# A spectral filter's middle stage: one sum per step on GpSimd, the last steps in another order, step 15 in two PSUM tiles, no transposes

## The chip, the cores and the metric

The kernel runs on one core of a Trainium2 chip. Its engines work beside each other, each through its own queue in program order: TensorE (PE, with its weight loads PEld) multiplies matrices into PSUM, VectorE (DVE) and ScalarE (ACT) read and write both SBUF and PSUM, GpSimd (POOL) works on SBUF, and SyncE (SP) issues the transfers between HBM and SBUF here. The metric is the time of one execution on the device in microseconds (us); less is better.

## The reference

All tensors are float32; x has 2048 rows of 576.

```python
def _A_ref(x, w_r, w_i):
    B, S, D = x.shape                      # 1, 2048, 576
    X = jnp.fft.rfft2(x, axes=(-2, -1))
    X = X * (w_r + 1j * w_i)               # 2048 x 289
    return jnp.fft.irfft2(X, s=(S, D), axes=(-2, -1))

def _B_ref(x, w1, w2):                     # 576 x 4608, 4608 x 576
    return jnp.maximum(x @ w1, 0) @ w2

h = x + _A_ref(_layernorm(x), A_w_r, A_w_i)
out = h + _B_ref(_layernorm(h), B_w1, B_w2)
```

## The kernel before

The program is straight-line code; the Python loops are unrolled, and what is written first on an engine runs first on it. It has four parts in time.

1. *Forward* (to about 33 us): layer norm of x and the first half of the two-dimensional transform, 16 row tiles; the result lies in the SBUF tile A (`zx`).
2. *Middle* (33 to 96 us; lines 385 to 460): 16 steps p = 0 to 15, each for two of 32 groups of frequencies. This is where the change lies.
3. *Inverse* (from 96 us): the way back, two row tiles per turn, with the second layer norm behind it and, from turn 5 on, the first units of the MLP. The loop is in lines 1043 to 1069.
4. *MLP* (to the end): matrix products of float32 values split in a high and a low part.

A middle step p consists of four functions, named here l, d, b and i with the step's number:

- l, `mid_l` (lines 390 to 396), for an even step and the next one together: products of the leftover rows of the transform, into a PSUM tile per step.
- d, `mid_d` (398 to 408): the main products of the transform along the row, into the same PSUM tile; one ACT copy of it to SBUF (128x580).
- b, `mid_b` (410 to 426): products for the second transform into PSUM; then on DVE two products with the filter W, `pr` and `pi` (L418 and L419, 128x578 each, read from PSUM), and four sums of 64x289 that make Y (L424: two differences of `pr`; L425: two sums of `pi`). Y holds two halves e = 0, 1 in its columns; each half needs one L424 and one L425. In steps 14 and 15 the difference of e = 0 and the sum of e = 1 run on POOL.
- i, `mid_i` (428 to 443): the first inverse product, 12 matmuls for each half e of Y, into one PSUM tile `pu`, then four ACT copies (128x160, L158) into the tile X (`U`), from which the inverse stage reads. Every row tile of the inverse needs columns of all 16 steps.

Line 155 is the helper that records all these matmuls, line 158 the helper of all ACT copies.

The loop of lines 445 to 460 runs d of step i, b of step i - 1 and i of step i - 2 in turn. At its end the order is:

```
turn 12: l12 d12 b11 i10      turn 15: d15 b14 i13
turn 13: d13 L b12 i11        turn 16: b15 S0 i14
turn 14: l14 d14 b13 i12      turn 17: S1 W8 i15, then W12
```

L is `load_weights(0, ...)` (line 349): a POOL memset of the tile G, one transfer of w1 columns (L337), three small ones into G (L339) and one of w2 rows (L347), all on SP. S0 and S1 are `split_weights(0, 0)` and `split_weights(0, 1)` (line 359): each makes high parts by ACT copies and low parts by DVE subtractions (L357, L381), for w1 and w2 of the first MLP group. W8 and W12 are 8 and 12 transposes of the identity on PE (`warm_pe`, line 297, L300), whose results nobody reads.

Behind the middle stage, SP issues 16 transfers that bring x back into the tile A (L472). They may start when d15 has read A for the last time. On PE the inverse starts with products that read U; on DVE with L535, L536 and L539 for each row tile (ACT copies first, POOL does L538), then L517 adds the residual for two row tiles.

Two allocators matter. `ebuf` hands out 10 SBUF buffers of tag e: each step takes four (one in d; `pr`, `pi` and Y in b), L two, S1 two. `ps` hands out four PSUM tiles of tag d: one per step from l, one in b, one in i.

Of the kernel before, what the change touches and what calls it, by code (L numbers as in the profile page):

```python
# [16 lines left out]
S, D, DFF = 2048, 576, 4608  # L17
NK = D // 2 + 1
NT = 16
NP = 16  # L20
# [102 lines left out]
def dims(ap, off, *pairs):  # L123

    return bass.AP(tensor=ap.tensor, offset=ap.offset + off, ap=[list(ap.ap[0]), *[list(p) for p in pairs]])
# [3 lines left out]
def kernel(ctx: ExitStack, tc: tile.TileContext, x, w_r, w_i, w1, w2, cc2, c1, fb, ib, c3, out):  # L129
    nc = tc.nc  # L130
# [5 lines left out]
    def sb(shape, tag, bufs=1, dt=F32):  # L136
        n[0] += 1
        return pool.tile(shape, dt, tag=tag, name=f"{tag}_{n[0]}", bufs=bufs)
# [3 lines left out]
    def ps():  # L142
        n[0] += 1
        if banks:
            return banks[0].tile([128, 1024], F32, tag="w", name=f"w_{n[0]}", bufs=2)
        return psum.tile([128, 1024], F32, tag="d", name=f"d_{n[0]}", bufs=4)
# [3 lines left out]
    def ebuf(shape, dt=F32):  # L150
        e = sb([128, EW], "e", EB, dt)[:, :int(np.prod(shape[1:]))]
        return e.rearrange("p (a b) -> p a b", a=shape[1]) if len(shape) == 3 else e

    def mm(o, l, r, start, stop):
        nc.tensor.matmul(o, l, r, start=start, stop=stop)  # L155

    def act(o, i, **kw):
        nc.scalar.activation(o, i, AF.Copy, **kw)  # L158
# [138 lines left out]
    def warm_pe(k):  # L297
        wm = ps()
        for _ in range(k):
            nc.tensor.transpose(wm[:, :128], ident, ident)  # L300
# [40 lines left out]
    def leftover():  # L341
        v4 = sb([128, 2, 256], "G")
        nc.gpsimd.memset(v4, 0.0)
        return v4
# [4 lines left out]
    def load_weights(g, v4):  # L349
        v1, v2 = ebuf([128, 4, 256]), ebuf([128, 2, D])  # L350
        raw[g] = v1, v2, v4
        load_w1(g, v1, v4)
        load_w2(g, v2)

    def split(h, l, v, eng=nc.vector):
        act(h, v)
        eng.tensor_sub(l, v, h)  # L357

    def split_weights(g, part):
        if part:  # L360
            r = [tail[0][:, 5120 + k:6272 + k] for k in (0, 1152)] if g == 2 else [ebuf([128, 1152], F32R) for _ in range(2)]
            h, l = (v.rearrange("p (a n) -> p a n", a=2) for v in r)
            wts[g, 1] = h, l
            split(h, l, raw[g][1], nc.gpsimd if g == 1 else nc.vector)
            return
        if g < 2:
            r = tail[0][:, 5120:7680] if g else sb([128, 2560], "F", dt=F32R)
            r = r[:, :1280], r[:, 1280:]
        else:
            r = [ebuf([128, 1280], F32R) for _ in range(2)]  # L370
        h, l = (v[:, :1024].rearrange("p (a n) -> p a n", a=4) for v in r)
        rest = [v[:, 1024:] for v in r]
        wts[g, 0] = h, l, rest
        v1, _, v4 = raw[g]
        split(h, l, v1, nc.gpsimd if g == 1 else nc.vector)
        for k in range(2):
            split_rest(rest[k], v4[:, k])

    def split_rest(o, v, eng=nc.vector):
        act(o, v)  # L380
        eng.tensor_sub(o[32:64], v[32:64], o[32:64])  # L381
# [3 lines left out]
    U = sb([128, 160 * 64], "X")  # L385
# [4 lines left out]
    def mid_l(*ps_):  # L390
        for p in ps_:
            Px[p] = ps()
            for e in range(2):
                q, z = slice(64 * e, 64 * e + 64), 8192 + 64 * (p + 16 * e)
                for r in range(2):
                    mm(Px[p][64 * r:64 * r + 64, 512 * e:512 * e + 290], zx[q, z:z + 64], lfv[q, r, :], True, False)

    def mid_d(p):
        px = Px.pop(p)
        for e in range(2):  # L400
            zt = [dims(zx, 2048 * b + 64 * (p + 16 * e), [1, 64]) for b in range(4)]
            o = [px[64 * r:64 * r + 64, 512 * e:512 * e + 290] for r in range(2)]
            for h in range(2):
                for r in range(2):
                    mm(o[r][:, 145 * h:145 * h + 145], zt[2 * r + h], cmv[:, 2 * r + h, :], False, h == 1)
        xx = ebuf([128, 2, 290])
        act(dims(xx, 0, [290, 2], [1, 2], [2, 145]), dims(px, 0, [512, 2], [145, 2], [1, 145]))
        Xs[p] = xx

    def mid_b(p):  # L410
        xx = Xs.pop(p)
        pz = ps()
        for c in range(2):
            for e in range(2):
                mm(pz[64 * e:64 * e + 64, 512 * c:512 * c + NK], FB[:, p, e, 64 * c:64 * c + 64], xx[:, e, :NK], True, True)
        zz = pz.rearrange("p (r n) -> p r n", r=2)[:, :, :NK]
        pr, pi = ebuf([128, 2, NK]), ebuf([128, 2, NK])
        nc.vector.tensor_mul(pr, zz, W[:, p])  # L418
        nc.vector.tensor_mul(pi, zz, dims(W, (2 * p + 1) * NK, [-NK, 2], [1, NK]))  # L419
        Y = ebuf([128, 2, NK])  # L420
        for e in range(2):
            q = slice(64 * e, 64 * e + 64)
            end = p >= NP - 2
            (nc.gpsimd if end and not e else nc.vector).tensor_sub(Y[:64, e], pr[q, 0], pr[q, 1])  # L424
            (nc.gpsimd if end and e else nc.vector).tensor_add(Y[64:, e], pi[q, 0], pi[q, 1])  # L425
        Ys[p] = Y

    def mid_i(p):
        Y = Ys.pop(p)
        pu = ps()  # L430
        for e in range(2):
            ibe = IB[p // 4][:, p % 4, e, :]
            for h in range(2):
                for g in range(2):
                    mm(pu[64 * g:64 * g + 64, 512 * e + 128 * h:512 * e + 128 * h + 128],
                       dims(Y, NK * e + 128 * g + h, [2, 64]), ibe, True, True)
            for g in range(2):
                mm(pu[64 * g:64 * g + 64, 512 * e + 256:512 * e + 320],
                   dims(Y, NK * e + 225, [1, 64]), ibe[:, 64 * g:64 * g + 64], True, True)
        for e in range(2):  # L440
            for j in range(2):
                act(dims(U, 64 * j + 32 * e + 2 * p, [128, 5], [640, 16], [1, 2]),
                    dims(pu, 512 * e + 2 * j, [64, 5], [4, 16], [1, 2]))

    for i in range(NP + 2):
        if i < NP:
            if i % 2 == 0:
                mid_l(i, i + 1)
            mid_d(i)
        if i == NP - 3:  # L450
            load_weights(0, leftover())
        if 1 <= i <= NP:
            mid_b(i - 1)
        if i >= NP:
            split_weights(0, i - NP)
        if i >= 2:
            if i > NP:
                warm_pe(8)
            mid_i(i - 2)
    warm_pe(12)  # L460
    xa = sb([128, 10240], "A")
    xs = xa[:, :NT * D].rearrange("p (t d) -> p t d", t=NT)
    sums = xa[:, NT * D:]
# [710 lines left out]
```

## Time and profile before

| | us |
|---|---|
| median of 3 runs (987.02 to 987.12) | 987.11 |
| the profiled execution | 987.22 |
| its span, first to last instruction | 985.1 |

| stretch of the span, us | what runs |
|---|---|
| 44.42 to 81.57 | ten middle steps, 7.43 for each two |
| 81.57 to 90.04 | l14 and d14 to b15 on TensorE |
| 90.26 to 96.19 | i14, W8, i15, W12 on TensorE |
| 96.12 to 131.13 | inverse, turns 0 to 5, before the first long MLP product |

A profile row is read as follows. In the timeline: start, duration (of the first to the last end of a merged group), engine, line, operation, what is written and read by tile names, shape and count; in brackets the engine's idle time before it, and what ended that. In the groups of instructions: busy time and mean duration in ns, then idle time. The releaser is inferred; TensorE's matmul ends are modelled, so its busy time hides short waits, and start-to-start times are the better measure there.

### The profile page before, as it was taken

The numbers are of one execution on the slowest core, as the hardware profiler recorded it, in microseconds if no ns is written. First come the engines' busy times: TensorE is split into PE (matmuls) and PEld (weight loads), VectorE is DVE, ScalarE is ACT, GpSimd is POOL, SyncE is SP. The second block draws the span as 40 slices with busy tenths as digits, with TensorE's granted clock in tenths as the row PEclk, the third lists the DMA queues.
The fourth block names the chain that finished last, engine by engine and source line by source line (L and its number), as shares of the span: only waits on it lengthen the run. The fifth ranks groups of instructions, "written<-read, shape, count | busy, mean of one in ns | idle before, by whom it ended". The sixth has DMA issues, their size and how long they took to land.

```text
span 985.1 us, 18082 instructions
## 1 busy us (share of the span) xinstructions
PE 970.2 (98%) x6700; PEld 859.7 (87%) x6700; DVE 758.5 (77%) x1200; ACT 454.6 (46%) x886; POOL 588.9 (60%) x724
## 2 busy tenths in 40 slices
PE   8999999999999999999999999999999999999997
PEld 7787678899998899999999999999999999999997
DVE  7688877347664888888788888888888888878886
ACT  6544365313233444445454444445444554544441
POOL 6201565402254868776777768686677777687741
PEclk9999999999999999999999999999999999999999
DMA  8865524546698281817456381918365462819365
GB/s 234 214 168 148 127 84 144 175 142 233 218 352 288 94 296 46 299 55 266 141 180 204 118 278 44 312 45 284 102 220 167 155 233 89 288 39 316 106 209 145
DMA packets 123607, 178.71 MB, mean 181 GB/s; under 512 B 7808, under 2 KB 102656, under 8 KB 123520
## 3 DMA queue, kind: packets, MB, share of 16 engines
q1 hardware_dynamic: 122640, 176.58, 55.5%
q8 instruction: 53, 0.87, 0.4%
q10 hardware_dynamic: 880, 0.98, 0.3%
q14 instruction: 34, 0.28, 0.1%
HBM read 153.15 MB, written 23.07 MB: 179 GB/s over the span
## 4 chain that ended last, share of the span: by engine, by line
PE 92%; DVE 4%; DMA 2%; ACT 1%; issue 1%; SPq 0%; POOL 0%; ACTq 0%; DVEq 0%
PE h L807 34%; PE w L912 33%; PE d L155 23%; DMA A<-in_A_x_dram 2%; PE d L559 1%; PE w L155 1%; DMA X<-in_A_x_dram 0%; DVE A L922 0%; DVE st L243 0%; DVE A L517 0%; PE h L912 0%; DVE st L216 0%; DVE e L264 0%; DVE D L623 0%; ACT D L622 0%
## 5 line engine op out<-in xcount | busy, mean ns | idle before, releaser
L922 DVE TENSOR_TENSOR A<-A,w 128x576 f32<-128x576 f32 x415 | 307.0, 751 | 84.6 <-PE w L912 71.5
L912 PE MATMUL w<-X,D 128*128 128x288 f32 x1416 | 217.5, 295 | 0.4 <-ACT e L626 0.3
L912 PEld LDWEIGHTS w<-X,D 128*128 128x128 f32 x1416 | 204.6, 188 | 10.5 <-ACT e L626 0.5
L807 PE MATMUL h<-B,e 128*128 128x512 f32 x630 | 160.2, 393 | 0.9 <-DVE A L616 0.9
L158 ACT ACTIVATE e<-h 128x512 f32<-128x512 f32 x90 | 53.9, 598 | 185.0 <-PE h L807 185.0
L807 PEld LDWEIGHTS h<-B,e 128*128 128x128 f32 x630 | 113.2, 188 | 20.8 <-ACT e L158 1.1
L357 POOL TENSOR_TENSOR e<-e,e 128x512 fp32r<-128x512 f32 (+3 forms) x61 | 78.3, 1284 | 58.0 <-ACT e L158 52.7
L807 PE MATMUL h<-X,e 128*128 128x512 f32 x420 | 106.1, 392 | 0.0
L626 ACT ACTIVATE e<-e 128x512 f32<-128x512 f32 x90 | 57.0, 633 | 105.8 <-DVE e L865 46.6
L357 POOL TENSOR_TENSOR X<-e,X 128x576 fp32r<-128x576 f32 (+1 forms) x32 | 46.9, 1467 | 73.3 <-ACT X L158 73.3
L807 PEld LDWEIGHTS h<-X,e 128*128 128x128 f32 x420 | 75.7, 188 | 12.8
L158 ACT ACTIVATE e<-e 128x256 fp32r<-128x256 f32 (+5 forms) x162 | 74.6, 489 | 22.3 <-DVE e L669 11.1
L831 POOL TENSOR_TENSOR A<-e 128x256 f32<-128x256 f32 x59 | 46.4, 787 | 27.7 <-DVE X L821 27.7
L821 DVE TENSOR_TENSOR D<-A,D 128x512 fp32r<-128x512 f32 x59 | 60.2, 1020 | 0.9 <-ACT D L158 0.9
L912 PEld LDWEIGHTS w<-X 128*128 128x128 f32 x360 | 53.8, 188 | 5.5 <-issue 0.7
L912 PE MATMUL w<-X 128*128 128x288 f32 x360 | 57.0, 294 | 0.5 <-DVE A L922 0.5
L912 PE MATMUL w<-X,e 128*128 128x288 f32 x348 | 55.5, 295 | 0.0
L807 PE MATMUL h<-F,e 128*128 128x512 f32 x210 | 53.7, 394 | 0.0
L155 PEld LDWEIGHTS d<-e,D 128*128 128x128 f32 x384 | 52.4, 188 | 1.2 <-issue 0.2
L155 PE MATMUL d<-e,D 128*128 128x288 f32 x384 | 53.4, 296 | 0.0
L807 PE MATMUL h<-C,e 128*128 128x512 f32 x210 | 53.2, 392 | 0.0
L833 POOL TENSOR_TENSOR A<-e,A 128x256 f32<-128x256 f32 x59 | 51.3, 870 | 0.8 <-DVE A L829 0.8
(168 smaller groups left out, 1859.6 us busy)
## 6 DMA issues: line engine op xcount, KB each, us to landing
X<-t0T SPq DMA_DIRECT2D x16, 768.0 KB, 8.1
X<-t1T SPq DMA_DIRECT2D x16, 768.0 KB, 7.7
e<-in_B_w_dram SPq DMA_DIRECT2D x18, 576.0 KB, 3.9
e<-in_B_w_dram SPq DMA_DIRECT2D x18, 512.0 KB, 3.7
X<-t0T SPq DMA_DIRECT2D x16, 512.0 KB, 8.6
X<-t1T SPq DMA_DIRECT2D x16, 512.0 KB
B<-t0T SPq DMA_DIRECT2D x8, 768.0 KB
F<-t0T SPq DMA_DIRECT2D x8, 768.0 KB
```

Of the source, the lines that this page charges most:

```text
L155: nc.tensor.matmul(o, l, r, start=start, stop=stop)
L158: nc.scalar.activation(o, i, AF.Copy, **kw)
L357: eng.tensor_sub(l, v, h)
L559: nc.tensor.transpose(pz[:, 128 * ORDER[b]:128 * ORDER[b] + 128], y[:, 128 * b:128 * b + 128], ident)
L626: nc.scalar.activation(o, i, AF.Relu)
L807: nc.tensor.matmul(o, a, b, start=bool(first) and n_ == 0, stop=n_ == len(ops) - 1, skip_group_check=not first)
L821: (eng or nc.vector).tensor_sub(f[1], v, f[0])
L831: nc.gpsimd.tensor_sub(s3, p0[:, :256], p0[:, 256:])
L833: nc.gpsimd.tensor_sub(s4, p1_[:, :256], s2)
L912: nc.tensor.matmul(P[tt], l[:, q], r, start=first and n_ == 0, stop=end and n_ == 2, skip_group_check=whole and not first)
L922: nc.vector.tensor_add(xt, xt, P)
```

## The change

In every step, Y's difference of half e = 0 goes to POOL and the other three sums stay on DVE, in another order: both sums of `pi`, then the difference of e = 1. The loop runs to turn 12 as before; what follows is written out. Each i from 11 on comes behind a later b. L comes behind b13 and i11. Step 15 puts its halves in two PSUM tiles, copies each half out as soon as it is done, and of each half's two copies one runs on DVE. S0 and S1 come behind i15. The 20 transposes are gone. In the string, `d13` stands for `mid_d(13)`, `l14` for `mid_l(14, 15)`, and so on.

```diff
--- before.py
+++ after.py
@@ -418,17 +418,25 @@
         nc.vector.tensor_mul(pr, zz, W[:, p])
         nc.vector.tensor_mul(pi, zz, dims(W, (2 * p + 1) * NK, [-NK, 2], [1, NK]))
         Y = ebuf([128, 2, NK])
+        q = [slice(64 * e, 64 * e + 64) for e in range(2)]
+        nc.gpsimd.tensor_sub(Y[:64, 0], pr[q[0], 0], pr[q[0], 1])
         for e in range(2):
-            q = slice(64 * e, 64 * e + 64)
-            end = p >= NP - 2
-            (nc.gpsimd if end and not e else nc.vector).tensor_sub(Y[:64, e], pr[q, 0], pr[q, 1])
-            (nc.gpsimd if end and e else nc.vector).tensor_add(Y[64:, e], pi[q, 0], pi[q, 1])
+            nc.vector.tensor_add(Y[64:, e], pi[q[e], 0], pi[q[e], 1])
+        nc.vector.tensor_sub(Y[:64, 1], pr[q[1], 0], pr[q[1], 1])
         Ys[p] = Y
 
     def mid_i(p):
         Y = Ys.pop(p)
-        pu = ps()
+        last = p == NP - 1
+        pus = [ps(), ps()] if last else [ps()] * 2
+
+        def evict(e, j, eng=None):
+            o = dims(U, 64 * j + 32 * e + 2 * p, [128, 5], [640, 16], [1, 2])
+            v = dims(pus[e], 512 * e + 2 * j, [64, 5], [4, 16], [1, 2])
+            eng.tensor_copy(o, v) if eng else act(o, v)
+
         for e in range(2):
+            pu = pus[e]
             ibe = IB[p // 4][:, p % 4, e, :]
             for h in range(2):
                 for g in range(2):
@@ -437,27 +445,32 @@
             for g in range(2):
                 mm(pu[64 * g:64 * g + 64, 512 * e + 256:512 * e + 320],
                    dims(Y, NK * e + 225, [1, 64]), ibe[:, 64 * g:64 * g + 64], True, True)
-        for e in range(2):
-            for j in range(2):
-                act(dims(U, 64 * j + 32 * e + 2 * p, [128, 5], [640, 16], [1, 2]),
-                    dims(pu, 512 * e + 2 * j, [64, 5], [4, 16], [1, 2]))
-
-    for i in range(NP + 2):
-        if i < NP:
-            if i % 2 == 0:
-                mid_l(i, i + 1)
-            mid_d(i)
-        if i == NP - 3:
+            if last:
+                evict(e, 0)
+                evict(e, 1, nc.vector)
+        if not last:
+            for e in range(2):
+                for j in range(2):
+                    evict(e, j)
+
+    for i in range(NP - 3):
+        if i % 2 == 0:
+            mid_l(i, i + 1)
+        mid_d(i)
+        if i >= 1:
+            mid_b(i - 1)
+        if i >= 2:
+            mid_i(i - 2)
+    for step in "d13 b12 l14 d14 b13 i11 L d15 b14 i12 b15 i13 i14 i15 S0 S1".split():
+        k = int(step[1:] or 0)
+        if step[0] == "l":
+            mid_l(k, k + 1)
+        elif step[0] == "L":
             load_weights(0, leftover())
-        if 1 <= i <= NP:
-            mid_b(i - 1)
-        if i >= NP:
-            split_weights(0, i - NP)
-        if i >= 2:
-            if i > NP:
-                warm_pe(8)
-            mid_i(i - 2)
-    warm_pe(12)
+        elif step[0] == "S":
+            split_weights(0, k)
+        else:
+            dict(d=mid_d, b=mid_b, i=mid_i)[step[0]](k)
     xa = sb([128, 10240], "A")
     xs = xa[:, :NT * D].rearrange("p (t d) -> p t d", t=NT)
     sums = xa[:, NT * D:]
```

## The prediction

> **What bounds the kernel now.** I read four views in this order: the page's busy times and its chain, a table of busy time by stretches, the timeline around the end of the middle stage, and the groups of transfers. Steps are named as above: l, d, b and i with the step's number, S0 and S1 for the weight splits, L for the weight load.
>
> ```profile
> PE 970.2 (98%) x6700; PEld 859.7 (87%) x6700; DVE 758.5 (77%) x1200; ACT 454.6 (46%) x886; POOL 588.9 (60%) x724
> ...
> PE 92%; DVE 4%; DMA 2%; ACT 1%; issue 1%; SPq 0%; POOL 0%; ACTq 0%; DVEq 0%
> ```
>
> TensorE sets nearly the whole time. The change can only win where TensorE waits or runs work that is not needed, so the question is where that is.
>
> ```profile
> 81.57:89.00 7.43, 7.43 (x118) 6.00 (x116) 6.32 (x13) 3.22 (x10) 0.00 (x0) 1.00 0.21 68
> ...
> 96.12:102.76 6.64, 6.64 (x66) 5.10 (x65) 4.14 (x8) 1.24 (x3) 1.56 (x2) 1.00 1.06 220
> 102.76:112.50 9.74, 8.25 (x83) 4.48 (x82) 9.40 (x23) 3.06 (x6) 4.63 (x8) 1.00 0.74 156
> 112.50:131.10 18.60, 17.62 (x156) 12.41 (x156) 17.01 (x43) 11.57 (x21) 13.84 (x25) 1.00 0.25 87
> ```
>
> Columns: the stretch, its length, then busy time of PE, PEld, DVE, ACT and POOL with counts, the granted clock, the DMA share and GB/s. Two middle steps last 7.43 us and PE is busy all of it, while DVE has 1.11 us free and POOL does nothing. So the steady loop is bound by PE. From 102.76 on it is the other way: DVE is busy 9.40 of 9.74 us and PE waits. The inverse stage opens bound by DVE, and stays close to it until about 131 us. What counts is therefore how early DVE can start that stage. TensorE, start to start:
>
> ```profile
> 79.39 1.14 PE L155 MATMUL d<-e,C 128*64 128x289 f32 x8
> ...
> 80.36 1.28 PE L155 MATMUL d<-D,e 128*64 128x128 f32 x24
> ...
> 81.57 2.35 PE L155 MATMUL d<-e,A 64*64 64x290 f32 x32
> ...
> 83.75 1.14 PE L155 MATMUL d<-e,C 128*64 128x289 f32 x8
> ...
> 84.72 1.27 PE L155 MATMUL d<-D,e 128*64 128x128 f32 x24
> ...
> 85.83 1.16 PE L155 MATMUL d<-e,A 128*64 128x145 f32 x16
> ...
> 86.82 1.14 PE L155 MATMUL d<-e,C 128*64 128x289 f32 x8
> ...
> 88.90 1.14 PE L155 MATMUL d<-e,C 128*64 128x289 f32 x8
> ...
> 90.26 1.65 PE L155 MATMUL d<-D,e 128*64 128x128 f32 x24 [0.22 <-DVE e L425]
> ...
> 91.84 1.09 PE L300 MATMUL d<-ident 128*128 128x128 f32 x8
> ...
> 94.66 1.53 PE L300 MATMUL d<-ident 128*128 128x128 f32 x12
> ...
> 96.12 6.71 PE L155 MATMUL d<-e,X 64*64 64x290 f32 x64
> ```
>
> These are b12, i11, l14 with d14, b13, i12, d15, b14, b15, i14, the two groups of transposes, and the start of the inverse. They give l+d 2.18, b 0.97, i 1.11, d 0.99. Between b15's end (90.04) and 96.12 there are only i14 and i15, 2.2 us of work: some 3.9 us are waits and transposes. The other engines in that stretch:
>
> ```profile
> 84.94 0.76 DVE L418 TENSOR_TENSOR e<-d,B 128x578 f32<-128x578 f32 x1 [0.92 <-PE d L155]
> ...
> 88.20 0.76 DVE L418 TENSOR_TENSOR e<-d,B 128x578 f32<-128x578 f32 x1
> ...
> 89.11 0.69 POOL L424 TENSOR_TENSOR e<-e 64x289 f32<-64x289 f32 x1 [58.23 <-DVE e L418]
> ...
> 89.66 0.46 DVE L425 TENSOR_TENSOR e<-e 64x289 f32<-64x289 f32 x1
> 89.87 0.81 POOL L425 TENSOR_TENSOR e<-e 64x289 f32<-64x289 f32 x1
> 89.87 1.08 ACT L158 ACTIVATE F<-e 128x1024 fp32r<-128x1024 f32 x1
> 90.15 0.84 DVE L424 TENSOR_TENSOR e<-e 64x289 f32<-64x289 f32 x1
> ...
> 91.02 0.76 DVE L418 TENSOR_TENSOR e<-d,B 128x578 f32<-128x578 f32 x1
> ...
> 92.97 0.83 DVE L424 TENSOR_TENSOR e<-e 64x289 f32<-64x289 f32 x1
> ...
> 93.84 1.23 DVE L357 TENSOR_TENSOR F<-e,F 128x1024 fp32r<-128x1024 f32 x1
> ...
> 94.77 0.90 ACT L158 ACTIVATE X<-d 128x160 f32<-128x160 f32 x4 [0.88 <-PE d L155]
> ...
> 95.88 1.36 DVE L357 TENSOR_TENSOR e<-e,e 128x1152 fp32r<-128x1152 f32 x1
> ...
> 98.55 0.41 ACT L158 ACTIVATE e<-d 128x290 f32<-128x290 f32 x1 [2.89 <-PE d L155]
> 99.07 0.46 DVE L535 TENSOR_TENSOR e<-e,d 128x288 f32<-128x288 f32 x1 [1.83 <-ACT e L158]
> ...
> 101.40 0.46 DVE L539 TENSOR_TENSOR X<-e 128x289 f32<-128x289 f32 x1
> ...
> 102.39 0.45 DVE L535 TENSOR_TENSOR e<-e,d 128x288 f32<-128x288 f32 x1 [0.53 <-ACT e L158]
> ```
>
> DVE runs the products of steps 14 and 15 from 88.20 to 93.80, the splits from 93.84 to 97.24, idles 1.83 us, does the first two inverse tiles from 99.07 to 101.86, and idles 0.53 us. The 2.36 us of idle time is the most that an earlier start of the inverse on PE can give back. From 102.39 DVE leads.
>
> **The change part by part.** *One sum on GpSimd in every step.* DVE's step is 3.26 us now (84.94 to 88.20: two products, four sums). With three sums, I take the tail's rows, where a sum already runs on POOL: the first DVE sum starts 1.46 after L418 (88.20 to 89.66), the next 0.49 later (90.15), so a step is 1.46 + 3 x 0.49 = 2.93. In steps 0 to 12 this buys nothing: PE needs 3.72 per step either way (7.43/2). POOL's sum starts 0.15 after L418 ends, lasts 0.69 and lies beside L419; it is done before the first sum of DVE. If that cover were gone it would still have 3.72 - 2.93 = 0.79 us to spare per step.
>
> The price that is in doubt is the wait of DVE behind POOL. Two rows show one: L424 takes 0.84 and 0.83 beside a POOL sum, against 0.46 for its neighbour L425. But L425 at 89.66 starts at once beside the POOL sum that ends at 89.80. Bounds for the new first sum: 0 and 0.39 per step; I take 0, because it stands where this L425 stands, behind the same POOL sum. In the sum below only the last two steps count, so the far end is 0.78. [...]
>
> *Last steps reordered.* TensorE's work up to i15 stays the same, in another order. From 80.36 (end of b12, where i11 stood): l14 and d14 from 80.46 (0.1 for the change of tile shape, as i takes 1.21 ahead of l), b13 at 82.64, i11 83.61, d15 84.72, b14 85.71, i12 86.68, b15 87.79, i13 88.76, i14 89.87, free at 90.97. DVE starts a product 1.19 after its b (83.75 to 84.94): step 13 at 83.83, done 86.76; step 14 at 86.90, done 89.83; step 15 could start at 88.98 but follows at 89.83. Its first DVE sum ends at 89.83 + 1.46 + 0.46 = 91.75, its last at 89.83 + 1.46 + 0.98 + 0.46 = 92.73, against 93.80 now. So PE, free at 90.97, waits for DVE: i15's first half starts at 91.89 (0.14 after its sum, as 90.12 to 90.26), the second at about 92.87.
>
> *Step 15 in two PSUM tiles, half of its copies on DVE.* From the last sum to the first copy of what it produced takes 0.97 now (93.80 to 94.77): 93.70. Only the second half's two copies are then left, one on ACT (0.90/4, some 0.31 alone), one on DVE. No DVE copy of this shape stands in these rows; its bounds are the ACT copy's share of 0.22 and, as the far end, the 0.76 of a whole product. Both are free, since DVE must wait for the split's high part anyway (next paragraph), and the inverse starts on PE at about 94.1 (94.5 with the far end).
>
> *Transposes out.* 1.09 + 1.53 us of PE go. They lay beside waits: without them PE waits instead.
>
> *Splits behind i15.* This takes back half. S0's first ACT copy (1.08 us) ran at 89.87 in a gap; now it queues behind the last eviction, from 93.90 (0.2 after the copy's start) to 94.98. The split's DVE subtraction starts 0.1 later (as 98.96 to 99.07), at 95.08, and S0 with S1 occupies DVE for 3.40 (93.84 to 97.24), to 98.48. Behind it in DVE's queue stands the first L535 of the inverse: 98.51, where PE alone would have allowed 94.1 + 2.95 = 97.05. The two tiles take 2.79, so the third tile's L535 comes at 101.33 instead of 102.39. PE and ACT have delivered it by then (94.1 + 102.39 - 96.12 = 100.4).
>
> The moved load, past b13 and i11 and behind POOL's sum of step 13 on POOL's queue (its memset), needs these rows:
>
> ```profile
> 30.35 0.52 POOL L343 MEMSET G<- 128x512 f32 x1
> ...
> 77.27 1.38 SPq L339 DMA_DIRECT2D G<-in_B_w_dram  x3
> ...
> 87.03 13.74 SPq L472 DMA_DIRECT2D A<-in_A_x_dram  x16
> ...
> A<-in_A_x_dram SPq DMA_DIRECT2D x16, 288.0 KB, 9.7
> ...
> e<-in_B_w_dram SPq DMA_DIRECT2D x1, 576.0 KB, 5.2
> ```
>
> POOL's sum 13 ends about 85.4, the memset 86.0, the three small transfers leave until 87.5, the w2 load at 87.6, and the reload of x queues behind it on SP from 88.0, not 87.03. w2 lands at 92.8 and is wanted by ACT behind S0's copies, not before 94.98; the first rows of x land by 97.7 (88.0 + 9.7) and are wanted by L517, behind the third tile's L535 at 101.33. Both are hidden, with 2.2 and 3.6 us to spare.
>
> **Sum.** 102.39 - 101.33 = 1.06 us. DVE and the engines that follow it carry this through to 131 us, where PE takes over, and it stays. The profiled execution took 987.22 (span 985.1 and 2.1 around it), 0.11 over the median: 987.22 - 1.06 = 986.16 for it, 986.05 for the median. I say 986.0.
>
> **The rivals.** *The splits don't hold DVE.* Then PE decides, with 96.12 - 94.1 = 2.0: 985.1. For it speaks DVE's idle time of 2.36; against it the order in ACT's queue. Chance 0.14. A further 0.05 for gains beyond it, if the steady steps hold small waits that PE's modelled ends hide.
>
> *POOL holds DVE up* as L424 at 90.15: 0.39 in steps 14 and 15, 986.05 + 0.78 = 986.8. Chance 0.12.
>
> *The gain is swallowed*, because the later reload of x, or another chain before 131 us, ends last all the same: 987.1. The landing times above speak against it. Chance 0.08.
>
> *The clock falls* once the transposes no longer fill PE's waits: slower.
>
> ```profile
> L300 PE MATMUL d<-ident 128*128 128x128 f32 x28 | 6.0, 412 | 1.4 <-POOL ident masks.py:199 1.4
> ```
>
> The kernel's first 28 transposes took 6.0 us, 0.21 each, against 1.53/12 = 0.13 at 94.66: 1.7 times as long. At that rate the 5.75 us of PE work up to the third inverse tile (102.39 - 96.12, less the 0.53 for ACT) become 9.8; it decides as soon as PE loses 0.9 us, and with 4.0 lost L535 comes at 104.4, 2.0 later than now: 989.1. Against it: PE waited 1.49 us in 102.76 to 112.50 with the clock at 1.00, and the longest new wait of PE, for the sum on POOL that closes the second inverse tile, is some 1.4. Chance 0.05. [...]
>
> *The w2 load lands late*, behind other traffic, as the reload's transfers do (9.7 instead of 5.2): 97.3, so that S1 starts 2 us late on ACT, and as DVE has 0.3 of that to spare, the third tile's L535 comes at 103.0: 987.7. It takes the gain from a landing at some 96.7 on. It is issued into an idle queue, ahead of that reload. Chance 0.04.
>
> **How the numbers follow.** The forecast has 0.52. Its own spread is some 0.5 us, as it is a chain of ten waits of 0.1 each and three durations. The range that holds 8 in 10 runs from a little beyond the PE-bound case to just above no change: 984.6 to 987.4. With 0.2% (2.0 us, about what a measurement can tell here), faster needs less than 985.1: half of the first rival, the 0.05, and a tail of the forecast make 0.23. Slower needs 989.1: 0.07. The rest, 0.70, is within.
>
> **What would show it.** In the changed profile: about 2.93 us from one L418 to the next in the last three steps, with no POOL wait ahead of the first sum; i15 in two pieces near 91.9 and 92.9; the inverse starting on PE at about 94.1 and the first L535 at 98.5, with the split of w2 right ahead of it and no idle time between. A first L535 near 97 would put the PE-bound case in its place; a clock under 1.00 in 91 to 103 us the slow one; a first L517 that waits for a transfer, the swallowed gain. The forecast is wrong if the steps before 80 us are not 3.72 long, or if DVE has idle time ahead of the third inverse tile.

## The result, and the profile after

The changed kernel took 985.65 us in the median of 22 runs (984.92 to 986.53), the kernel before 987.05 (22 runs, 986.18 to 987.62): a ratio of 0.9987 with a 95% interval of 0.9981 to 0.9993. The gain is 1.40 us; 1.06 was forecast, and 986.0 for the time. The profiled execution's span is 983.7 us against 985.1.

The timeline of the changed kernel over the end of the middle stage. Its lines are numbered a little higher: L422 is the sum on POOL, L424 and L425 are DVE's sums, L436 DVE's copies of step 15, L548 the first DVE operation of an inverse tile (L535 before), L530 the residual add (L517 before), L485 the transfers that bring x back (L472 before).

```profile
83.93 0.76 DVE L418 TENSOR_TENSOR e<-d,B 128x578 f32<-128x578 f32 x1 [0.41 <-PE d L155]
...
84.84 0.69 POOL L422 TENSOR_TENSOR e<-e 64x289 f32<-64x289 f32 x1 [2.64 <-DVE e L418]
...
85.39 0.94 DVE L424 TENSOR_TENSOR e<-e 64x289 f32<-64x289 f32 x2
...
86.93 0.76 DVE L418 TENSOR_TENSOR e<-d,B 128x578 f32<-128x578 f32 x1
...
87.84 0.69 POOL L422 TENSOR_TENSOR e<-e 64x289 f32<-64x289 f32 x1 [1.85 <-DVE e L418]
...
88.46 0.94 DVE L424 TENSOR_TENSOR e<-e 64x289 f32<-64x289 f32 x2
88.54 0.39 SPq L347 DMA_DIRECT2D e<-in_B_w_dram  x1
...
89.03 15.22 SPq L485 DMA_DIRECT2D A<-in_A_x_dram  x16
...
89.93 0.76 DVE L418 TENSOR_TENSOR e<-d,B 128x578 f32<-128x578 f32 x1
...
92.06 0.78 PE L155 MATMUL d<-D,e 128*64 128x128 f32 x12 [0.87 <-DVE e L424]
92.43 0.46 DVE L425 TENSOR_TENSOR e<-e 64x289 f32<-64x289 f32 x1
...
93.03 0.78 PE L155 MATMUL d<-D,e 128*64 128x128 f32 x12 [0.20 <-DVE e L425]
93.22 0.33 DVE L436 COPY X<-d 128x160 f32<-128x160 f32 x1 [0.33 <-ACT X L158]
93.85 0.30 ACT L158 ACTIVATE X<-d 128x160 f32<-128x160 f32 x1 [0.66 <-PE d L155]
94.05 1.05 ACT L158 ACTIVATE F<-e 128x1024 fp32r<-128x1024 f32 x1
94.18 0.32 DVE L436 COPY X<-d 128x160 f32<-128x160 f32 x1 [0.64 <-ACT X L158]
...
94.20 7.06 PE L155 MATMUL d<-e,X 64*64 64x290 f32 x64 [0.39 <-ACT X L158]
...
95.13 1.23 DVE L357 TENSOR_TENSOR F<-e,F 128x1024 fp32r<-128x1024 f32 x1 [0.62 <-ACT F L158]
...
97.16 1.36 DVE L357 TENSOR_TENSOR e<-e,e 128x1152 fp32r<-128x1152 f32 x1
...
98.44 0.45 DVE L548 TENSOR_TENSOR e<-e,d 128x288 f32<-128x288 f32 x1
...
101.14 0.45 DVE L548 TENSOR_TENSOR e<-e,d 128x288 f32<-128x288 f32 x1
...
103.84 1.41 DVE L530 TENSOR_TENSOR A<-A,d 128x576 f32<-128x576 f32 x2
```

Read from the bottom: the third inverse tile starts on DVE at 101.14 without idle time before it, the first at 98.44 right behind the w2 split, that split behind the w1 split, and the w1 split at 95.13, after 0.62 us of waiting for ACT's copy at 94.05. That copy stood behind ACT's last eviction at 93.85, which waited for i15's second half. In the kernel before, DVE was idle ahead of the first and the third tile; here these gaps are gone. Three others have come between DVE's last sum and the splits, 0.33 and 0.64 ahead of its two copies and 0.62 ahead of the w1 split: 1.59 us in place of 2.36.

| | before | forecast | after |
|---|---|---|---|
| step 14 on DVE (L418) | 88.20 | 86.90 | 86.93 |
| step 15 on DVE | 91.02 | 89.83 | 89.93 |
| i15's first half on TensorE | 93.09 | 91.89 | 92.06 |
| inverse starts on TensorE | 96.12 | 94.1 | 94.20 |
| w1 split on DVE | 93.84 | 95.08 | 95.13 |
| first inverse tile on DVE | 99.07 | 98.51 | 98.44 |
| third inverse tile on DVE | 102.39 | 101.33 | 101.14 |

The stretches of the changed kernel (length, then busy time of PE, PEld, DVE, ACT and POOL, clock, DMA share and GB/s):

```profile
44.42:51.85 7.43, 7.43 (x116) 5.93 (x112) 5.59 (x11) 3.24 (x10) 1.38 (x3) 1.00 1.04 252
...
102.76:112.50 9.74, 8.52 (x81) 4.51 (x73) 9.43 (x24) 2.64 (x5) 4.54 (x8) 1.00 0.99 214
```

TensorE is still busy all of the 7.43 us, and from the first filter product of step 0 (37.14) to b12 on TensorE (79.42) 42.28 us pass, against 42.29 before: the steps of the loop kept their length. The inverse still opens with DVE busy nearly throughout. The last two residual adds of the whole program, before and after, in the timeline:

```profile
979.23 1.54 DVE L922 TENSOR_TENSOR A<-A,w 128x576 f32<-128x576 f32 x2 [1.69 <-PE w L912]
```

```profile
977.99 1.54 DVE L935 TENSOR_TENSOR A<-A,w 128x576 f32<-128x576 f32 x2 [1.69 <-PE w L925]
```

1.24 us lie between them, as 1.25 did between the third tiles (102.39 and 101.14): what was won by 101 us went through 877 us of other work unchanged. The other 0.2 us between the spans come behind these adds.

### The profile page after: what moved, and what is told of

Its sections match the earlier page's. It is cut to its first block, busy times and chain, and to the rows that moved or that the text cites. A ratio compares the mean times of both kernels' runs of the same rounds, so it can differ in the third digit from the quotient of the medians.

```text
span 983.7 us, 18061 instructions
## 1 busy us (share of the span) xinstructions
PE 968.0 (98%) x6680; PEld 857.8 (87%) x6680; DVE 754.4 (77%) x1190; ACT 454.3 (46%) x884; POOL 597.1 (61%) x736
## 4 chain that ended last, share of the span: by engine, by line
PE 92%; DVE 5%; ACT 1%; issue 1%; DMA 0%; POOL 0%; ACTq 0%; DVEq 0%; POOLq 0%
PE h L820 34%; PE w L925 33%; PE d L155 23%; PE w L155 1%; PE d L572 1%; DVE st L243 1%; DMA X<-in_A_x_dram 0%; DVE e L549 0%; DVE A L935 0%; DVE e L548 0%; DVE X L552 0%; DVE e L264 0%; PE h L925 0%; POOL B L582 0%; DVE A L530 0%
```

## The experiments

Single executions differ by up to 0.5 us in the forward stage, before the change has any part in it. So each profile is compared by the time from the first filter product of step 0 (37.10 in the kernel before) to the start of the last residual add (980.02, the second of the two in its row above). The table has one profiled execution each. The only kernel that was profiled twice without a fall of the clock, split_early_two, gave 940.96 and 940.97.

| kernel | first product | last add | between | against changed |
|---|---|---|---|---|
| before | 37.10 | 980.02 | 942.92 | +1.28 |
| changed | 37.14 | 978.78 | 941.64 | 0 |
| sum_alone | 37.15 | 980.00 | 942.85 | +1.21 |
| sums_back | 37.34 | 979.08 | 941.74 | +0.10 |
| transposes_back | 37.11 | 978.95 | 941.84 | +0.20 |
| one_tile | 37.07 | 979.22 | 942.15 | +0.51 |
| copies_on_act | 37.45 | 979.24 | 941.79 | +0.15 |
| order_back | 37.31 | 981.83 | 944.52 | +2.88 |
| order_back_act | 37.31 | 981.01 | 943.70 | +2.06 |
| split_early | 37.33 | 980.06 | 942.73 | +1.09 |
| split_early_again | 36.98 | 978.14 | 941.16 | -0.48 |
| split_early_two | 37.32 | 978.28 | 940.96 | -0.68 |
| split_early_two_timed | 37.15 | 978.12 | 940.97 | -0.67 |
| split_early_keep | 37.48 | 978.40 | 940.92 | -0.72 |

The theory (A): the reordered end of the middle stage makes the gain, and the splits, now behind i15, take a part of it back. The rivals: the sum on POOL makes it (B), the transposes (C), the splits don't hold the inverse (D), the tiles and transposes without the order (E).

**sum_alone**: the kernel before with the new sums.

```diff
+        q = [slice(64 * e, 64 * e + 64) for e in range(2)]
+        nc.gpsimd.tensor_sub(Y[:64, 0], pr[q[0], 0], pr[q[0], 1])
         for e in range(2):
-            q = slice(64 * e, 64 * e + 64)
-            end = p >= NP - 2
-            (nc.gpsimd if end and not e else nc.vector).tensor_sub(Y[:64, e], pr[q, 0], pr[q, 1])
-            (nc.gpsimd if end and e else nc.vector).tensor_add(Y[64:, e], pi[q, 0], pi[q, 1])
+            nc.vector.tensor_add(Y[64:, e], pi[q[e], 0], pi[q[e], 1])
+        nc.vector.tensor_sub(Y[:64, 1], pr[q[1], 0], pr[q[1], 1])
```

> The kernel before with the new sums alone (one on POOL in every step, three on DVE, also in steps 14 and 15). Theory A (the reordered last steps make the gain, the sum on POOL buys nothing while PE bounds the loop): the middle loop keeps 7.43 us for two steps; in the last two steps DVE now has three sums instead of two beside POOL, so step 15 ends about 0.4 later (94.2 instead of 93.80), the inverse starts on PE at about 96.5 instead of 96.12, and the whole is 0.3 to 0.5 us slower than before. Theory B (the sum off DVE makes the gain): the whole is 1.0 to 1.4 us faster than before.

Measured: 986.94 us, and 0.07 us less than before in the trace. B falls. The kernel before took 988.31 in its one execution beside this run, and by that pair alone B would have come true; but 988.31 lies above every other execution of it on record (986.18 to 987.93), it has no trace, and the three runs that follow, made beside the same execution, took 985.85 to 986.01, about 1 us less than this one. A's size was a miss too: nothing was lost. Its timeline at step 15:

```profile
93.46 0.46 DVE L425 TENSOR_TENSOR e<-e 64x289 f32<-64x289 f32 x1
...
96.14 1.21 PE L155 MATMUL d<-e,X 64*64 64x290 f32 x16
```

Step 15's last sum ends at 93.92, not 94.2: a step with three sums took 2.90 here, not the 3.00 of the changed kernel, and the step with two sums beside POOL that it replaces took 2.82. The inverse starts at 96.14 against 96.12.

**sums_back**: the changed kernel with the sums as before.

```diff
-        q = [slice(64 * e, 64 * e + 64) for e in range(2)]
-        nc.gpsimd.tensor_sub(Y[:64, 0], pr[q[0], 0], pr[q[0], 1])
         for e in range(2):
-            nc.vector.tensor_add(Y[64:, e], pi[q[e], 0], pi[q[e], 1])
-        nc.vector.tensor_sub(Y[:64, 1], pr[q[1], 0], pr[q[1], 1])
+            q = slice(64 * e, 64 * e + 64)
+            end = p >= NP - 2
+            (nc.gpsimd if end and not e else nc.vector).tensor_sub(Y[:64, e], pr[q, 0], pr[q, 1])
+            (nc.gpsimd if end and e else nc.vector).tensor_add(Y[64:, e], pi[q, 0], pi[q, 1])
```

> The changed kernel with the sums as before (four on DVE up to step 13, then two on POOL in steps 14 and 15). Theory A: step 13 takes 3.26 on DVE and delays step 14 by some 0.2, steps 14 and 15 take 2.82 each instead of 3.00; the end of step 15's sums moves by -0.2 to 0, and the whole is within 0.3 us of the changed kernel. Theory B: it loses the gain, 1.0 us or more slower than the changed kernel.

Measured: 986.01 us, 0.10 behind the changed kernel. Step 15's sums end 0.12 later in it (93.21, less the 0.20 by which it began later, against 92.89), where A had 0 to 0.2 earlier. The sum on POOL in every step, the largest edit by count, is worth 0.1 us at most.

**transposes_back**: 8 transposes ahead of i15 and 12 behind it.

```diff
-    for step in "... b15 i13 i14 i15 S0 S1".split():
+    for step in "... b15 i13 i14 W8 i15 W12 S0 S1".split():
...
+        elif step[0] == "W":
+            warm_pe(k)
```

> The changed kernel with 8 transposes ahead of i15 and 12 behind it, as before. Theory A (they cost only what PE has no wait for): the 8 lie beside PE's wait of 0.87 ahead of i15 and cost 0 to 0.2; the 12 take 1.5 behind i15 and start the inverse on PE at about 95.5 instead of 94.2, of which DVE's splits hide the first two tiles; the third tile's first subtraction comes about 0.5 later (101.6 instead of 101.14), and the whole is 0.4 to 0.7 slower than the changed kernel. Theory C (the transposes were the price, the rest is nothing): 1.2 or more slower. A clock under 1.00 in the changed kernel that these bring back would make it faster; none is expected, both at 1.00.

Measured: 985.85 us, 0.20 behind. In its timeline:

```profile
91.09 1.09 PE L300 MATMUL d<-ident 128*128 128x128 f32 x8
...
92.11 1.58 PE L155 MATMUL d<-D,e 128*64 128x128 f32 x24
...
93.63 1.53 PE L300 MATMUL d<-ident 128*128 128x128 f32 x12
...
95.09 2.15 PE L155 MATMUL d<-e,X 64*64 64x290 f32 x22
```

The 8 fill the wait of 0.87 and push i15 by 0.05. The 12 begin at 93.63, earlier than I had counted, and start the inverse at 95.09, 0.89 late. DVE's splits hide all but 0.2 of it, where A had 0.4 to 0.7. C falls: 2.6 us of TensorE work cost 0.2.

**one_tile**: step 15 in one PSUM tile, its four copies on ACT behind both halves.

```diff
-        pus = [ps(), ps()] if last else [ps()] * 2
+        pus = [ps()] * 2
...
-            if last:
-                evict(e, 0)
-                evict(e, 1, nc.vector)
-        if not last:
-            for e in range(2):
-                for j in range(2):
-                    evict(e, j)
+        for e in range(2):
+            for j in range(2):
+                evict(e, j)
```

> The changed kernel with step 15 in one PSUM tile and its four copies on ACT behind both halves, as before. Theory A (ACT's queue sets when the splits, and so the inverse on DVE, start): the first copy starts at 93.85 as now, the split's first ACT copy 0.55 to 0.7 later (94.7 instead of 94.05), and the whole is 0.5 to 0.7 slower than the changed kernel. Rival D (the inverse is not held by the splits): PE starts the inverse 0.5 later but has slack, and the whole is within 0.2.

Measured: 985.87 us, 0.51 behind. The timeline shows the path:

```profile
93.70 0.89 ACT L158 ACTIVATE X<-d 128x160 f32<-128x160 f32 x4 [1.64 <-PE d L155]
...
94.45 1.08 ACT L158 ACTIVATE F<-e 128x1024 fp32r<-128x1024 f32 x1
```

Four copies of step 15 now stand ahead of the split's copy on ACT, where the changed kernel has two, and it comes at 94.45 and not at 94.05. TensorE started the inverse at 94.45 too, 0.32 later than in the changed kernel counted from the first product, but had slack: DVE took up the third tile at 101.57 without idle time before it. If D held, the 0.51 would not have shown.

**copies_on_act**: two PSUM tiles, all four copies on ACT.

```diff
                 evict(e, 0)
-                evict(e, 1, nc.vector)
+                evict(e, 1)
```

> The changed kernel with all four copies of step 15 on ACT (two PSUM tiles as changed). In the changed kernel each DVE copy began only when ACT's copy of the same half had ended (94.18 behind 93.85 + 0.30). Theory A: two ACT copies follow each other 0.2 apart, so the inverse starts on PE within 0.15 of the changed kernel or earlier, while the split's first ACT copy starts 0.2 later: the whole is 0.1 to 0.25 slower. Rival (the DVE copies run beside ACT's and save their time): 0.3 or more slower.

Measured: 986.16 us, 0.15 behind in the trace. The inverse starts on TensorE at 94.52. This execution's first filter product came 0.31 later than the changed kernel's; without that it is 94.21, as there. So the copies on DVE buy nothing on TensorE; they spare ACT one copy. Between this kernel and one_tile stand the two tiles, with the earlier copies of the first half that they allow: they are worth 0.36 of the 0.51.

**order_back** and **order_back_act**: the last steps, the load and the splits in the order of before, with all the rest as changed; in the second, step 15's copies on ACT.

```diff
-    for step in "d13 b12 l14 d14 b13 i11 L d15 b14 i12 b15 i13 i14 i15 S0 S1".split():
...
+    for i in range(NP + 2):
+        if i < NP:
+            if i % 2 == 0:
+                mid_l(i, i + 1)
+            mid_d(i)
+        if i == NP - 3:
+            load_weights(0, leftover())
+        if 1 <= i <= NP:
+            mid_b(i - 1)
+        if i >= NP:
+            split_weights(0, i - NP)
+        if i >= 2:
+            mid_i(i - 2)
```

> The changed kernel with the last steps, the weight load and the splits in the order of before; no transposes, two PSUM tiles for step 15, the new sums. Theory A: DVE takes up step 14 at 88.1 and step 15 at 91.0 as in the kernel before (86.93 and 89.93 in the changed one), the splits' ACT copies run in early gaps, the inverse starts on PE at 95.2 to 95.5 and PE, not DVE, sets its third tile: 101.5 to 101.8, so 0.4 to 0.7 slower than the changed kernel. Theory E (two tiles and no transposes are the gain, the order nothing): within 0.2 of the changed kernel.

> order_back with all copies of step 15 on ACT, so that none stands behind the splits on DVE. In order_back those DVE copies ran at 97.43, behind the splits, and held PE's inverse until 98.03. Theory A: without them the inverse starts on PE at 95.4 to 95.6 in one piece, PE sets the third tile at 101.6 to 102.0 against 101.14, and the whole is 0.4 to 0.8 slower than the changed kernel and 0.5 to 0.9 faster than before. Rival E (the order itself is worth nothing): within 0.2 of the changed kernel.

Measured: 988.90 us and 2.88 behind; 987.88 us and 2.06 behind. Both are dearer than expected, each for a reason of its own. In order_back the DVE copies of step 15 stand behind the splits in DVE's queue, and the inverse waits for them:

```profile
96.15 1.36 DVE L357 TENSOR_TENSOR e<-e,e 128x1152 fp32r<-128x1152 f32 x1
97.43 0.55 DVE L436 COPY X<-d 128x160 f32<-128x160 f32 x2
98.03 0.69 PEld L155 LDWEIGHTS d<-e,X 64*64 64x64 f32 x14 [2.44 <-DVE X L436]
```

So DVE's part in the copies needs the splits behind i15. In order_back_act step 15 and the inverse start as expected:

```profile
91.19 0.76 DVE L418 TENSOR_TENSOR e<-d,B 128x578 f32<-128x578 f32 x1
...
95.40 8.53 PE L155 MATMUL d<-e,X 64*64 64x290 f32 x64 [0.40 <-ACT X L158]
```

Less the 0.17 by which this execution's first product came later, DVE takes up step 15 1.09 later and TensorE the inverse 1.03 later than in the changed kernel. Then the clock falls. The stretches around that:

```profile
92.25:95.66 3.41, 1.81 (x28) 1.59 (x31) 3.25 (x6) 2.75 (x9) 0.47 (x1) 1.00 1.06 228
95.66:99.08 3.42, 3.42 (x21) 2.25 (x20) 1.82 (x3) 0.00 (x0) 0.00 (x0) 0.50 1.06 228
```

What such a fall costs was measured on another kernel (1.57 us, next). Less that, order_back_act stands 0.49 behind the changed kernel, within what A expected; this is an estimate from two runs, as the kernel was not run without a fall. A second estimate does without that price: in split_early_again, whose clock held, the third tile came 6.44 behind the start of the inverse (94.05 to 100.49), which here gives 101.84, 0.53 later than the changed kernel's after the same 0.17. E would have the order change nothing. The rows ahead of the fall speak against it, but the size of the order's part is estimated, and it holds the 0.15 of the copies on ACT.

**split_early**, **split_early_again**: the w1 split ahead of i15, the copies of step 15 on ACT; the second is the same kernel once more.

```diff
-    for step in "... b15 i13 i14 i15 S0 S1".split():
+    for step in "... H0 b15 i13 i14 R0 i15 S1".split():
...
+        elif step[0] == "H":
...
+            act(h, raw[0][0])
+        elif step[0] == "R":
+            for j in range(2):
+                act(rest[j], raw[0][2][:, j])
+            nc.vector.tensor_sub(l, raw[0][0], h)
+            for j in range(2):
+                nc.vector.tensor_sub(rest[j][32:64], raw[0][2][32:64, j], rest[j][32:64])
```

> The changed kernel with the w1 split ahead: its large ACT copy behind the copies of i12 (a gap of ACT from 88.9 to 90.1), its small ones behind those of i14, its DVE subtractions behind step 15's sums (92.9 on, where DVE waits 2.2 us); all four copies of step 15 on ACT; the w2 split stays behind i15. Theory A (the splits hold DVE at the opening of the inverse): DVE has done them by 97, the first subtraction of the inverse comes at 97.2 to 97.5 instead of 98.44, the third tile is then set by PE at about 100.7 instead of 101.14, and the whole is 0.4 to 0.6 faster than the changed kernel. Rival D (they don't hold it): no more than 0.1 faster.

> The kernel split_early unchanged, once more. In its first run the granted clock was 0.50 from 94.7 to 98.1 and the third tile's subtraction came at 102.47 with the first at 99.10. Theory F (the fall depends on where a window of the clock gate happens to lie over PE's waits around i15, not on the kernel alone): with the clock at 1.00 the first subtraction comes at 97.2 to 97.6 and the third at 100.5 to 100.9; the times of the runs spread over two values some 1.5 apart. Rival G (the kernel always brings the fall): again 0.50 at the same place and 102.4.

Measured: 986.74 us in the one execution of the first; 985.09 (984.39 to 985.61, 10 runs) for the second, ratio 0.9978 (0.9969 to 0.9987). Here are the stretches of the two, each from 3.11 us before the inverse starts on TensorE (94.40 and 94.05). First split_early:

```profile
91.29:94.70 3.41, 1.93 (x33) 1.63 (x33) 3.18 (x6) 2.67 (x11) 0.43 (x1) 1.00 1.03 293
94.70:98.12 3.42, 3.42 (x22) 2.23 (x21) 1.78 (x3) 0.89 (x1) 0.00 (x0) 0.50 1.05 225
98.12:101.50 3.38, 3.38 (x34) 2.61 (x34) 2.26 (x6) 0.83 (x2) 0.88 (x1) 1.00 1.06 234
```

Then split_early_again:

```profile
90.94:94.35 3.41, 1.94 (x33) 1.63 (x32) 3.18 (x6) 2.67 (x11) 0.43 (x1) 1.00 1.05 257
94.35:97.77 3.42, 3.42 (x36) 2.71 (x38) 2.40 (x5) 1.41 (x3) 0.00 (x0) 1.00 1.05 217
```

One program, one pattern of waits (TensorE busy 1.93 and 1.94 of 3.41 us), and once half the clock for the next 3.41 us, once not. With the clock at half, 22 matmuls got through where 36 did. The whole difference, 942.73 - 941.16 = 1.57 us, is the price of one fall. G falls: the kernel does not always bring it. The two values some 1.5 apart that F expected did not come either: ten executions lie between 984.39 and 985.61.

That the place of a window decides was not tried by itself, but the clock records of the traces bear on it. Each opens where the clock first rises, at another time in each execution: at 6.99 us in the kernel before, 6.42 in the changed one (whose first transposes follow each other at 0.21 us up to 6.32 and at 0.11 from 6.48 on), 5.96 in split_early, 4.17 in split_early_again. The falls come a whole number of 3.413 us behind that: 26 of these in the two executions where it fell at the inverse (5.96 to 94.70 in split_early, 6.92 to 95.66 in order_back_act), and 286 in the kernel before and in the changed one, where the only fall comes behind the last matmul (6.99 to 983.20, 6.42 to 982.63). Laid out from there, the first stretch shown of split_early is one such window. In split_early_again, whose record opens at 4.17, the same waits are cut by the border of two windows:

```profile
89.50:92.92 3.42, 2.35 (x48) 2.13 (x45) 3.19 (x7) 2.82 (x13) 0.69 (x1) 1.00 0.97 286
92.92:96.33 3.41, 3.01 (x35) 2.31 (x36) 2.82 (x4) 1.86 (x5) 0.00 (x0) 1.00 1.07 228
```

This fits F. TensorE's busy time in a window can't be the whole rule, though. In order_back one window has less of it than either window ahead of a fall, and its clock stays at 1.00:

```profile
96.37:99.78 3.41, 1.75 (x19) 1.12 (x20) 1.61 (x3) 0.00 (x0) 0.00 (x0) 1.00 1.07 224
99.78:103.20 3.42, 3.42 (x35) 2.65 (x34) 2.14 (x5) 0.83 (x2) 0.88 (x1) 1.00 1.06 222
```

With the clock up, what theory A forecast for split_early comes out. The timeline of split_early_again:

```profile
97.12 0.46 DVE L561 TENSOR_TENSOR e<-e,d 128x288 f32<-128x288 f32 x1 [0.43 <-ACT e L158]
...
100.49 0.46 DVE L561 TENSOR_TENSOR e<-e,d 128x288 f32<-128x288 f32 x1 [0.58 <-ACT e L158]
```

DVE now waits again ahead of the first and third tile: TensorE sets the opening, and D falls. The kernel gains 0.48 on the changed one, and 0.63 on copies_on_act, from which it differs by the moved split alone.

**split_early_two** (run twice, the second time timed) and **split_early_keep**: a second sum of steps 14 and 15 on POOL; then also 6 transposes in TensorE's wait ahead of i15.

```diff
-        for e in range(2):
-            nc.vector.tensor_add(Y[64:, e], pi[q[e], 0], pi[q[e], 1])
+        nc.vector.tensor_add(Y[64:, 0], pi[q[0], 0], pi[q[0], 1])
+        (nc.gpsimd if p >= NP - 2 else nc.vector).tensor_add(Y[64:, 1], pi[q[1], 0], pi[q[1], 1])
...
-    for step in "... H0 b15 i13 i14 R0 i15 S1".split():
+    for step in "... H0 b15 i13 i14 W6 R0 i15 S1".split():
...
```

> split_early with a second sum of steps 14 and 15 on POOL (the sum of half e = 1). Theory A: DVE's steps 14 and 15 shorten by what a sum takes, 0.46, less the wait of the last DVE sum for POOL's reads, 0.39, so by 0.1 to 0.2 each; i15's second half comes 0.2 to 0.4 earlier and the whole is 0.1 to 0.4 faster than split_early. Rival (POOL's second sum, behind its first, sets the end): POOL ends step 15 later than DVE does, no gain or a loss up to 0.3.

> The kernel split_early_two unchanged, timed. Its profile ended 0.5 earlier than the changed kernel's (last residual add 978.28 against 978.78, though its span began 0.18 later against the first product). Theory A: 1.7 to 2.0 faster than the kernel before in the median, with single runs 1.5 slower where the clock falls. Rival: no faster than the changed kernel's 1.4.

> split_early_two with 6 transposes in PE's wait ahead of i15 (0.77 to 0.88 us long; 6 take about 0.75). Theory F (they keep the window busy): no cost in a run without a fall (third tile within 0.1 of split_early_two's 100.64), no run with a fall, so 1.8 to 2.0 faster than the kernel before with a narrower spread than split_early_two. Rival H (transposes don't count as work for the clock): the same spread as split_early_two.

Measured: 985.54 us and, timed, 985.15 (984.76 to 985.81, 11 runs), ratio 0.9981 (0.9972 to 0.9990); with the transposes 985.17 (984.40 to 985.55, 11 runs), 0.9978 (0.9969 to 0.9987). The kernel before took 987.15 beside them (27 runs). In the trace the second sum gains 0.2, from the timeline of split_early_two:

```profile
89.14 0.84 DVE L425 TENSOR_TENSOR e<-e 64x289 f32<-64x289 f32 x1
90.01 0.76 DVE L418 TENSOR_TENSOR e<-d,B 128x578 f32<-128x578 f32 x1
```

The last DVE sum takes 0.84 beside POOL's second one, and still the step is shorter: 2.89 from 87.12 to 90.01, against 3.00. The transposes cost nothing (0.05 less than without, in one execution). Whether they prevent falls stays open: no profile of these kernels shows one, no single execution was 1.5 slower, and the spread of the times is about the same with and without (1.15 and 1.05 us), where F had it narrower. With the clock up, all three versions beat the changed kernel in the trace, by 0.5 to 0.7 us; by ratio the intervals overlap with its 0.9981 to 0.9993.

## Why the prediction was right

*What bounds what.* TensorE in the loop, DVE from the third inverse tile to 131 us, TensorE again behind: right. The loop kept its 7.43, and the 1.25 us won at the third tile arrived whole at the last add.

*The sum on POOL.* Right that it buys nothing in steps 0 to 12 (sum_alone -0.07, sums_back +0.10). Mis-sized: the step takes 3.00 (86.93 to 89.93), not 2.93, for the first sum starts 1.53 after L418 and not 1.46. Nothing in the trace shows POOL holding it. In step 13 the first sum starts 1.46 after L418 (83.93 to 85.39), 0.03 behind the end of L419, whose product it reads, and 0.14 before POOL's recorded end (84.84 + 0.69). In steps 14 and 15 the trace has a semaphore instruction of 0.02 us on DVE there, and the sum starts 0.07 behind that one's start. So of the two ends for DVE's wait behind POOL, 0 and 0.39, the 0 that I took came: the first sum started before POOL's recorded end in every step, by 0.06 to 0.14.

*The reordered steps.* Right to 0.2 us at every event of the table. TensorE waits 0.87 ahead of i15; about 0.9 was forecast. The load moved past two queues stayed hidden, though its last transfers left about 1 us later than forecast: w2 at 88.54 against 87.6, the reload of x at 89.03 against 88.0. The spare time of 2.2 and 3.6 covered that.

*Step 15 in two tiles.* The forecast for the eviction was 93.70, measured 93.85, the 0.15 being the two late DVE steps. The tiles matter (0.36), the copies on DVE less (0.15). I had them run beside ACT's; each began when ACT's copy of that half had ended (94.18, 93.85 + 0.30).

*Splits behind i15.* Right, and the term that the whole sum hung on: 98.51 forecast, 98.44 measured, and the experiment that moves one split ahead gives 0.48 back, 0.63 against copies_on_act. "Takes back half" was somewhat high: TensorE alone would have allowed a gain of some 1.9 (96.12 to 94.20), 1.25 came.

*The sum.* 1.06 forecast, 1.25 in the trace at the third tile. The difference lies in the first two inverse tiles: they took 2.70 from 98.44 to 101.14, where 2.82 (98.51 to 101.33) and a start 0.07 later had been counted. The prediction took DVE's two tiles to the end of their last record (99.07 to 101.86); in the timeline of before the second tile starts 1.36 behind the first (99.07 to 100.43), and twice that is 2.72. The 1.40 between the medians holds 0.15 more, which lies within the interval of the ratio.

*The parts.* Undone in one execution each, order with copies (0.49, estimated), tiles with copies (0.51), transposes (0.20) and sums (0.10) give 1.30, against 1.28 for the whole. The closeness is luck: the 0.15 of the copies is in it twice, and as TensorE sets the opening in some of these kernels and DVE in others, the parts need not add.

*The rivals.* That the splits don't hold DVE, that POOL holds it by 0.39, that the gain is swallowed, that the w2 load lands late (it landed 4.0 behind 88.54, ahead of the 92.8 forecast): none came. The clock rival did not come in the changed kernel's profile, but my reason against it was wrong. I judged by the length of the waits, 1.49 us in all in a stretch that kept its clock and some 1.4 for the longest new one. The runs disagree: the clock fell in two of the ten profiles without transposes ahead of the inverse, behind 3.41 us in which TensorE was busy for more than half (1.93 and 1.81 us) and no wait was over 1.3 us (0.88 and 1.26 at most). What does bring a fall stays open. The changed kernel has a like stretch, 1.95 of 3.40 us from 91.20, but the window of its profile, from 91.75, has 2.51 of 3.41. So the transposes that it drops may have been an insurance; no run shows that they prevent a fall. A fall would cost it about 1.1 by estimate, the 1.57 less the 0.5 by which TensorE is ahead of DVE at the third tile (94.20 + 6.44, against 101.14). One of its 22 executions may have paid: the one of 986.39 has a mean granted clock of 0.997, which otherwise only the two profiles with a fall show. No trace of it was kept.

## What to carry to other kernels

Where a stage opens bound by another engine, what counts is not when TensorE is free but when that engine's queue is: the splits behind the last eviction held it until 98.44, and putting one of them into a gap that the queues already had gained 0.48 more. An engine's idle time that ends in a wait gives an upper bound for the gain (2.36 here); the queue order behind the wait says how much of it comes. Dummy work beside a wait was nearly free here, and its removal gained little (0.20 for 2.6 us of TensorE work). Before taking it out, look at all the waits of a stretch and not at the longest alone: both falls of the clock came behind waits that were short one by one (0.88 and 1.26 at most).

## What the runs showed of the hardware

At the opening of the inverse the granted clock fell to 0.50 for 3.41 us twice (split_early, order_back_act), at once behind a stretch of 3.41 us with TensorE busy 1.93 and 1.81 us; the kernel of the first did not fall there in its other profiled run, split_early_again, where the two windows of 3.413 us over the same waits, counted from the opening of the clock record, had 2.35 and 3.01. In order_back a window with 1.75 brought no fall. One fall cost 1.57 us (split_early against split_early_again). A DVE sum of 64x289 between two SBUF operands started 0.14 us before the recorded end of a POOL sum of the same size (85.39 against 85.53, step 13 of the changed kernel).
